# A searched order, an earlier z and reordered loads in a linear-attention and gMLP block

## The chip, the cores and the metric

The kernel runs on one core of one Trainium2 chip. A core has five engines that run side by side, each through its own list of instructions in order: TensorE (PE) for matmuls, VectorE (DVE), ScalarE (ACT), GpSimd (POOL), and SyncE (SP), which here only issues transfers. They wait for each other through semaphores. The metric is the device time of one execution in microseconds; the median of several runs counts.

## The reference

x has 2048 tokens of 512 values in bf16. Two blocks follow each other, each after a layer norm and with a residual sum.

```python
phi = lambda t: jnp.where(t > 0, t + 1, jnp.exp(t)) + 1e-06
# A: 32 heads of 16
pq, pk = phi(q), phi(k)                      # q, k, v = layernorm(x) @ wqkv
kv  = einsum('bhsd,bhse->bhde', pk, v)
z   = einsum('bhsd->bhd', pk)
o   = einsum('bhqd,bhde->bhqe', pq, kv) / (einsum('bhqd,bhd->bhq', pq, z) + 1e-06)
h   = x + o @ wo
# B
y   = gelu(layernorm(h) @ w_in)              # 1792 columns, two halves of 896
z1, z2 = y[..., :896], layernorm(y[..., 896:])
g   = einsum('ts,bsf->btf', w_sp, z2) + b_sp[None, :, None]
out = h + (z1 * g) @ w_out
```

The sum over all tokens in kv and z means that no q can be used before the last k is done; the spatial product with w_sp (2048 x 2048) means that no g can be computed before the last z2 is normalised.

## The kernel before

Tokens are cut into NT = 16 tiles of 128, and for some steps into NG = 4 groups of 512. The kernel is written as a list of operations with their reads and writes (`_Prog.add`). Nothing in the source fixes the order in which an engine runs them: dependencies come from the footprints in memory, and `schedule` makes an order by a model. Each operation has a cost and a latency in nanoseconds, written where it is added (for instance 167 and 535 for the two POOL steps of `rstd`, lines 501 and 503). `_pass` is a list scheduler: at each step the engine that can start first takes its ready operation of best rank. `schedule` (line 166) ranks by the longest path to the end, then alternates passes forward and backward in time (ROUNDS = 12) and keeps the shortest plan. `emit` writes each engine's list in that order, with the waits that the dependencies need. Source order still matters in one way: two operations that share a buffer are ordered as the source has them.

The stages, with the names that the profile shows:

- Loads. `load_x` and `load_w` issue transfers on the queues of SP and ACT (line 438): x in pieces of one or two tiles, the weights wk (keys) and wq (queries), each 512 KB. Each has a latency for the model. POOL makes constants, and ACT loads the table for Exp and Ln (line 459) with a priority of 9e5.
- Warm-up. `warmup(40)` runs 40 matmuls on zeros (line 547) while the first loads are under way.
- `k_unit(n)` takes two tiles: statistics on DVE (`stats`, lines 495 and 496), the reciprocal deviation on POOL (`rstd`), the normalisation into xn on DVE or ACT, a transpose into xnT on PE (line 527, the first six tiles) or by DMA (line 441), the K product into one of the two pairs of PSUM banks 0-1 and 2-3, which `next_pair` hands out in turn, and `phi` into pk (ACT Exp, line 427 "e"; DVE, lines 539 and 540). Then xn^T pk is summed over all tiles in banks 4 to 7 (line 589, list CB). This is the matrix C from which kv follows as wv^T C, so v itself is never made.
- `q_unit(tg, c)` makes two of four blocks of 128 query columns for one group of 512 tokens, in a pair from `next_pair`, with `phi` into pqT. There are eight of these units. QS says after which k_unit how many are written down; the rest follow the transition.
- Transition. C goes to SBUF (ct, line 620). z comes from sixteen small matmuls on pk (line 626), an ACT copy (zsum), eight small matmuls with a selector (line 647) and four DVE steps into zmat (line 651); it uses bank ZB = CB[0]. kv is made in bank CB[1] (line 636), masked to the heads (kvm), and multiplied by wo into m (banks 6, 7, 5, 4; line 658).
- Denominators. For every group and pair of blocks, zmat^T pqT goes to banks 6 and 7, ACT takes Ln and then Exp of the negative (line 427 "r", one buffer), and DVE multiplies pqT (line 672).
- h tiles. pqT^T m goes to banks 4 and 5; then x is added (line 683), and statistics, rstd, normalisation into hn and a transpose by DMA into hnT follow.
- z2 and z1. After the last denominator ACT loads the Gelu table (line 694). z2 of a tile is hnT^T win (lines 702 and 705), Gelu, its layer norm in DVE and POOL steps (lines 714 to 722, 513). z1T is 28 tiles of win^T hnT with Gelu, in banks 6 and 7.
- G and output. For each of four groups, seven products of z2 with the transposed w_sp (448 matmuls in all), bias and product with z1T (lines 763 and 765), and the output product with wout (line 753).

Of the kernel before, what the change touches and what calls it, by code (L numbers as in the profile page):

```python
# [6 lines left out]
ACT = mybir.ActivationFunctionType  # L7
ALU = mybir.AluOpType

P = 128  # L10
GRAN = 16
SEM_NS = 45.0
LOOK = 100.0
ROUNDS = 12


class _Op:
# [13 lines left out]
class _Prog:  # L31
# [98 lines left out]
    def _pass(self, rank, back):  # L130
# [32 lines left out]
                    cand[ops[u].eng].append(u)  # L163
        return start

    def schedule(self):
        ops = self.ops
        for o in ops:
            for d in o.deps:
                ops[d].users.append(o.i)  # L170
        for o in reversed(ops):
            o.prio = max((ops[u].prio + self._lag(o, ops[u]) for u in o.users), default=o.lat) + o.cost + o.bias
        rank = [-o.prio for o in ops]
        best = None
        for _ in range(ROUNDS):
            start = self._pass(rank, False)
            span = max(start[o.i] + o.cost + o.lat for o in ops)
            if best is None or span < best[0] - 1:
                best = (span, start)
            late = self._pass([-(start[o.i] + o.cost) for o in ops], True)  # L180
            rank = [-(late[o.i] + o.cost) for o in ops]
        self.est, self.start = best
        self.seq = sorted(ops, key=lambda o: (self.start[o.i], o.i))
        self.order = {e: [o for o in self.seq if o.eng == e] for e in self.ENGS}
# [91 lines left out]
def bass_sequential_preLN__linear_attn_block__mixer_gmlp__prompt_kernel(  # L276
# [11 lines left out]
    _, S, D = A_x.shape  # L288
# [4 lines left out]
    NT, KD, KF = S // P, D // P, FH // P  # L293
    GW = 512
# [6 lines left out]
    g = _Prog(nc)  # L301
# [37 lines left out]
    wqkv = g.sbuf("wqkv", o_wqkv, [KD, 3 * D], BF16)  # L339
# [4 lines left out]
    pk = g.sbuf("pk", o_pk, [NT, D], BF16)  # L344
# [12 lines left out]
    zsum = g.sbuf("zsum", o_r, [GW], FP32)  # L357
# [41 lines left out]
    def PE(fn, reads, writes, ns, **k):  # L399
        return g.add("PE", fn, reads, writes, cost=ns, lat=165, **k)  # L400
# [11 lines left out]
    def dve_cost(n, ps, acc=1):  # L412
        return n / acc / 0.96 + 58

    def act_cost(n, ps):
        return n / 1.2 + (49 if ps else 92)

    def act(out_ap, in_ap, func, n, bias=None, scale=None, extra=(), accum=None, **k):
        kw = {}
        if bias is not None:  # L420
            kw["bias"] = bias
        if scale is not None:
            kw["scale"] = scale
        if accum is not None:
            kw["accum_out"] = accum
        ps = in_ap.tensor.name == "psum"
        return g.add("ACT", lambda ac: ac.activation(out_ap, in_ap, func, **kw), [in_ap, *extra],  # L427
                     [out_ap] + ([accum] if accum is not None else []),
                     cost=act_cost(n, ps) + 93 * len(extra) + (92 if accum is not None else 0), lat=120, **k)

    def dve(fn, reads, writes, n, ps=False, acc=1, **k):
        return g.add("DVE", fn, reads, writes, cost=dve_cost(n, ps, acc), lat=95, **k)
# [4 lines left out]
    def dma(eng, out_ap, in_ap, name, issue=100.0, lat=2500.0, **k):  # L437
        return g.add(eng, lambda q: q.dma_start(out_ap, in_ap), [in_ap], [out_ap], cost=issue, lat=lat, dma=name, **k)

    def dma_t(out_ap, in_ap, name, issue=1310.0, lat=1600.0, **k):  # L440
# [15 lines left out]
                                   base=0, channel_multiplier=1), [bmask], [bmask], 350, bias=1e5)  # L456
    pool(lambda p: p.affine_select(bm3, bm3, pattern=[[DH, P // DH], [0, DH]], compare_op=ALU.is_gt, fill=0.0,
                                   base=DH, channel_multiplier=-1), [bmask], [bmask], 350, bias=1e5)
    g.add("ACT", lambda ac: ac.preload_act_table_set("natural_log_exp_and_others"), [], [], cost=1300, bias=9e5)


    later = [1e6]
# [1 line left out]
    def prio():  # L464
        later[0] -= 1e3
        return later[0]

    wq = A_wqkv.rearrange("(c p) f -> p c f", p=P)

    def load_w(eng, j, nm, lat):  # L470
        dma(eng, wqkv[:, :, j * D:(j + 1) * D], wq[:, :, j * D:(j + 1) * D], nm, issue=500, lat=lat, bias=prio())

    def load_x(eng, n, w, lat):
        dma(eng, x[:, n:n + w, :], x_d[n * P:(n + w) * P, :].rearrange("(n p) d -> p n d", p=P), f"x{n}", issue=500,
            lat=lat, bias=prio())
# [3 lines left out]

    load_x("SP", 0, 1, 2000)  # L480
    load_x("ACT", 1, 1, 2200)
    load_w("SP", 1, "wk", 4300)
    load_x("ACT", 2, 2, 3000)
    load_x("ACT", 4, 2, 4000)
    load_x("SP", 6, 2, 5500)
    load_x("ACT", 8, 2, 5000)
    load_x("SP", 10, 2, 6500)
    load_x("ACT", 12, 2, 6000)
    load_x("SP", 14, 2, 7500)
    load_w("ACT", 0, "wq", 9000)  # L490


    def stats(src, k, n):
# [40 lines left out]
    def phi(dst, b, w=2):  # L534

        e, t = e_t[ecnt[0] % NE][:, 0:w, :], psum[:, b:b + w, :]
        ecnt[0] += 1
        act(e, t, ACT.Exp, w * GW)
        dve(lambda v: v.tensor_scalar(e, e, 1.0, EPS_PHI, op0=ALU.min, op1=ALU.add), [e], [e], w * GW, acc=4)  # L539
        dve(lambda v: v.scalar_tensor_tensor(dst, t, 1.0 + EPS_PHI, e, op0=ALU.add, op1=ALU.max),  # L540
            [t, e], [dst], w * GW, ps=True)

    def warmup(n):
        def fn(pe):
            inst = None
            for _ in range(n):
                inst = pe.matmul(bank(7, P), lhsT=warm, rhs=warm, start=True, stop=True)
            return inst
        PE(fn, [warm], [bank(7, P)], n * 64, bias=1e6)

    warmup(40)

    PAIRS = [0, 2]
    pc = [0]

    def next_pair():
        pc[0] += 1
        return PAIRS[pc[0] % 2]

    CB = [4, 5, 6, 7]  # L560
# [34 lines left out]
    def q_unit(tg, c):  # L595
        b = next_pair()
        for i in (0, 1):
            matmuls(bank(b + i), [(wqkv[:, d, (c + i) * P:(c + i + 1) * P], xnT[:, d, tg * GW:(tg + 1) * GW])
                                  for d in range(KD)])
        phi(pqT[:, c:c + 2, tg * GW:(tg + 1) * GW], b)  # L600

    QS = {8: 1, 10: 1, 12: 2, 14: 2}
    qs = [(tg, c) for tg in range(NG) for c in range(0, KD, 2)]
    for n in range(0, NT, 2):
        k_unit(n)
        for _ in range(QS.get(n, 0)):
            q_unit(*qs.pop(0))

    for dst, src, nm in ((wqkv[:, :, 2 * D:3 * D], A_wqkv[:, 2 * D:3 * D], "wv"), (wo, A_wo, "wo"),
                         (win, B_w_in, "win"), (wout, B_w_out, "wout")):  # L610
        late = load("SP", dst, src, nm, 2000, issue=src.shape[0] * src.shape[1] * 2 / 350)
        late.deps.add(g.last.i)


    ZB, KVB = CB[0], CB[1]
    for c in range(KD):
        if c % 2:
            act(ct[:, c, :], bank(CB[c]), ACT.Copy, GW)
        else:
            dve(lambda v, c=c: v.tensor_copy(ct[:, c, :], bank(CB[c])), [bank(CB[c])], [ct[:, c, :]], GW, ps=True)  # L620

    def fn(pe):
        inst = None
        for i in range(NT // 4):
            for j in range(4):
                inst = pe.matmul(psum[32 * j:32 * (j + 1), ZB, :], lhsT=ones32, rhs=pk[:, 4 * i + j, :],
                                 start=i == 0, stop=i == NT // 4 - 1)
        return inst
    PE(fn, [ones32, pk], [bank(ZB)], NT // 4 * 300)
    act(zsum, bank(ZB), ACT.Copy, GW)  # L630

    def fn(pe):
        inst = None
# [6 lines left out]
    dve(lambda v: v.tensor_tensor(kvm, bank(KVB).rearrange("p (c t) -> p c t", c=KD),  # L640
                                  bmask.rearrange("p (c t) -> p c t", c=1).to_broadcast([P, KD, P]), ALU.mult),
        [bank(KVB), bmask], [kvm], GW, ps=True)

    def fn(pe):
        inst = None
        for c in range(KD):
            inst = pe.matmul(bank(ZB, 1, c), lhsT=zsum[:, c * P:(c + 1) * P], rhs=sel[:, 0:1], start=True, stop=True)
        return inst
    PE(fn, [zsum, sel], [bank(ZB)], KD * 250)
    for c in range(KD):  # L650
        dve(lambda v, c=c: v.tensor_scalar(zmat[:, c, :], bmask, bank(ZB, 1, c), None, op0=ALU.mult),
            [bmask, bank(ZB)], [zmat[:, c, :]], P)
    for c, b in zip(range(KD), (6, 7, 5, 4)):
        matmuls(bank(b), [(kvm[:, c, :], wo[:, c, :])])
        if c % 2:
            act(m[:, c, :], bank(b), ACT.Copy, GW)
        else:
            dve(lambda v, c=c, b=b: v.tensor_copy(m[:, c, :], bank(b)), [bank(b)], [m[:, c, :]], GW, ps=True)
# [21 lines left out]
    for n in range(NT):  # L680
        b = AB[n % 2]
# [14 lines left out]
    for n in range(NT):  # L696
        b = next_pair()
# [34 lines left out]
    for tg in range(NG):  # L732
        for fc in range(KF):
            b = Z1B[k % 2]
# [22 lines left out]
    for tg in range(NG):  # L757
        tok = slice(tg * GW, (tg + 1) * GW)
        for fc in range(KF):
            b = GB[(tg * KF + fc) % 2]  # L760
            matmuls(bank(b), [(z2[:, s, fc * P:(fc + 1) * P], wsp[:, s, tok]) for s in range(NT)])
            t, z = u_t[fc % 2], z1T[:, fc, tok]
# [37 lines left out]
```

## Time and profile before

| | |
|---|---|
| time, median of 3 runs | 260.2 us (260.05 to 260.46) |
| span in the profile | 258.9 us |
| PE busy | 243.6 us (94%) |
| DVE busy | 132.7 us (51%) |
| ACT busy | 86.6 us (33%) |
| POOL busy | 46.5 us (18%) |
| mean granted clock of PE | 0.98 |
| POOL rs L501, 128x1, mean | 258 ns |
| POOL rs L503, 128x1, mean | 604 ns |
| ACT Ln, Exp of a denominator, mean | 1114, 1058 ns |
| DVE pk/pqT L540, 128x1024, mean | 1225 ns |

The profile is of one execution. Busy time is the union of an engine's instructions; matmuls overlap, so that a record of a 128x512 matmul is 379 ns long where the next one starts after 216 ns. The chain of waits is the sequence of work that ended last, followed back from the end: at each step to what released it. The granted clock is the share of PE's full clock that was let through.

### The profile page before, as it was taken

To read this page: it belongs to the slowest core of one execution; us is meant where nothing else is said; L and a number is where in the kernel's file an instruction comes from. 1 tells how busy PE (TensorE), PEld (TensorE's weight loads), DVE (VectorE), ACT (ScalarE), POOL (GpSimd) and SP (SyncE) were. 2 spreads that over 40 slices of the span, in tenths; PEclk is the share of its full clock that TensorE was granted. 3 is DMA by queue.
4 is the path that set the end of the run, shared out by engine and by line. 5 is a ranking of instruction groups with operands and counts; after the bars stand their busy time and mean duration, and the time that the engine had idled before them with its cause. 6 is when DMAs were issued, how large, how long until landed. Compare 5 with 4: busy or idle time off the path is not lost.

```text
span 258.9 us, 3119 instructions
## 1 busy us (share of the span) xinstructions
PE 243.6 (94%) x1180; PEld 111.7 (43%) x1180; DVE 132.7 (51%) x270; ACT 86.6 (33%) x122; POOL 46.5 (18%) x134
## 2 busy tenths in 40 slices
PE   5698999995989999799999999999999999999995
PEld 5343444451334454344444444444444444444442
DVE  2998665587699999982322221414204211054063
ACT  1379633469689667561000001103003000000020
POOL 5345100000136887960000000000000000000000
PEclk9799999998699999999999999999999999999999
DMA  7813479943034444684544444000000000021012
GB/s 226 261 41 81 85 242 368 121 102 81 1 78 88 95 87 101 85 167 98 93 92 101 101 85 100 20 0 3 0 0 0 0 3 0 0 81 61 22 61 101
DMA packets 57166, 21.57 MB, mean 83 GB/s; under 512 B 49472, under 2 KB 56512, under 8 KB 57152
## 3 DMA queue, kind: packets, MB, share of 16 engines
q1 hardware_dynamic: 55392, 19.67, 32.9%
q10 hardware_dynamic: 1760, 1.70, 2.0%
q8 instruction: 9, 0.15, 0.2%
q14 instruction: 5, 0.04, 0.1%
HBM read 7.47 MB, written 2.10 MB: 37 GB/s over the span
## 4 chain that ended last, share of the span: by engine, by line
PE 67%; DVE 15%; POOL 8%; ACT 5%; DMA 2%; issue 2%; POOLq 0%; ACTq 0%
PE psum L408 62%; POOL rs L503 5%; DVE st L495 4%; PE psum L589 4%; DVE h L683 2%; POOL rs L501 2%; ACT r L427 2%; DMA x<-in_A_x_dram 2%; DVE pk L540 2%; DVE hn L513 2%; ACT e L427 2%; DVE st L720 1%; DVE st L721 1%; DVE z L513 1%; DVE st L496 1%
## 5 line engine op out<-in xcount | busy, mean ns | idle before, releaser
L408 PE MATMUL psum<-wsp,z 128*128 128x512 bf16 x448 | 98.2, 379 | 0.2 <-DVE z L513 0.2
L408 PEld LDWEIGHTS psum<-wsp,z 128*128 128x128 bf16 x448 | 43.7, 98 | 53.3 <-DVE z L513 0.7
L427 ACT ACTIVATE z1T<-psum 128x512 bf16<-128x512 f32 x28 | 16.7, 597 | 121.8 <-PE psum L408 121.8
L763 DVE TENSOR_TENSOR u<-psum,bsp 128x512 bf16<-128x512 f32 x28 | 19.2, 690 | 39.7 <-PE psum L408 39.4
L765 DVE TENSOR_TENSOR z1T<-u,z1T 128x512 bf16<-128x512 bf16 x28 | 11.6, 421 | 40.1 <-ACT z1T L427 39.7
L408 PE MATMUL psum<-hnT,win 128*128 128x512 bf16 x112 | 26.3, 379 | 0.0
L503 POOL TENSOR_TENSOR rs<-rs,expo 128x1 f32<-128x1 f32 (+1 forms) x41 | 25.7, 628 | 2.4
L408 PE MATMUL psum<-wout,z1T 128*128 128x512 bf16 x112 | 25.3, 379 | 0.0
L427 ACT ACTIVATE e<-psum 128x1024 bf16<-128x1024 f32 (+1 forms) x18 | 16.6, 926 | 17.1 <-PE psum L408 17.1
L501 POOL TENSOR_SCALAR rs<-st 128x1 f32<-128x1 f32 (+1 forms) x41 | 10.4, 255 | 65.2 <-DVE st L496 62.0
L753 DVE TENSOR_TENSOR ost<-psum,h 128x512 bf16<-128x512 f32 x16 | 10.2, 683 | 19.3 <-PE psum L408 19.3
L702 PE MATMUL psum<-win,hnT 128*128 128x512 bf16 x64 | 16.4, 379 | 2.1 <-DMA hnT<-hn 2.0
L408 PE MATMUL psum<-m,pqT 128*128 128x512 bf16 x64 | 17.7, 420 | 0.7 <-DVE h L683 0.6
L427 ACT ACTIVATE z<-psum 128x896 bf16<-128x896 f32 x16 | 14.6, 910 | 10.7 <-PE psum L705 10.6
L408 PE MATMUL psum<-wqkv,xnT 128*128 128x512 bf16 x64 | 16.5, 399 | 1.2 <-ACT xnT L427 1.0
L408 PEld LDWEIGHTS psum<-wout,z1T 128*128 128x128 bf16 x112 | 11.0, 98 | 13.2
L408 PE MATMUL psum<-xnT,wqkv 128*128 128x512 bf16 x64 | 15.6, 379 | 0.7 <-DVE pk L540 0.7
L589 PE MATMUL psum<-pk,xn 128*128 128x512 bf16 x64 | 16.1, 379 | 0.0
L408 PEld LDWEIGHTS psum<-hnT,win 128*128 128x128 bf16 x112 | 10.2, 98 | 13.7 <-ACT z1T L427 3.2
L705 PE MATMUL psum<-win,hnT 128*128 128x384 bf16 x64 | 13.0, 326 | 0.0
L539 DVE TENSOR_SCALAR e<-e 128x1024 bf16<-128x1024 bf16 (+1 forms) x18 | 7.2, 398 | 11.3 <-ACT e L427 11.2
L495 DVE BATCH_NORM_STATS2 st<-x 128x6 f32<-128x512 bf16 x16 | 10.4, 679 | 4.9 <-DMA x<-in_A_x_dram 4.9
(67 smaller groups left out, 203.5 us busy)
## 6 DMA issues: line engine op xcount, KB each, us to landing
out_dram<-ost SPq DMA_DIRECT2D x16, 128.0 KB, 1.7
win<-in_B_w_in_dram SPq DMA_DIRECT2D x1, 1792.0 KB, 11.3
x<-in_A_x_dram ACTq DMA_DIRECT2D x4, 256.0 KB, 7.1
wqkv<-in_A_wqkv_dram SPq DMA_DIRECT2D x2, 512.0 KB, 4.7
wsp<-in_B_w_sp_dram SPq DMA_TRANSPOSE x64, 2.8
wout<-in_B_w_out_dram SPq DMA_DIRECT2D x1, 896.0 KB, 7.3
x<-in_A_x_dram SPq DMA_DIRECT2D x3, 256.0 KB, 6.9
wqkv<-in_A_wqkv_dram ACTq DMA_DIRECT2D x1, 512.0 KB, 8.9
```

What stands on the lines that cost most here:

```text
L408: inst = pe.matmul(out_ap, lhsT=a, rhs=b, start=start and i == 0, stop=stop and i == len(pairs) - 1)
L427: return g.add("ACT", lambda ac: ac.activation(out_ap, in_ap, func, **kw), [in_ap, *extra], [out_ap] + ([accum] if accum is not None else []),
L495: dve(lambda v: v.bn_stats(s[:, 0:6], src[:, n, :]), [src[:, n, :]], [s[:, 0:6]], D)
L501: pool(lambda p: p.tensor_scalar(rr[:, :, 1:2], ss[:, :, col + 1:col + 2], EPS_LN, None, op0=ALU.add), [ss[:, :, col + 1:col + 2]], [rr], 167)
L503: pool(lambda p: p.tensor_tensor(rr[:, :, 0:1], rr[:, :, 1:2], expo[:, 0:w].rearrange("p (a b) -> p a b", b=1), ALU.pow), [rr, expo], [rr] ...
L513: dve(lambda v: v.tensor_scalar(dst, src, mean, rst, op0=ALU.subtract, op1=ALU.mult), [src, mean, rst], [dst], w + 460, acc=4)
L589: inst = pe.matmul(bank(CB[c]), lhsT=xn[:, i, c * P:(c + 1) * P], rhs=pk[:, i, :], start=i == 0, stop=i == NT - 1)
L702: pe.matmul(bank(b), lhsT=hnT[:, c, n * P:(n + 1) * P], rhs=win[:, c, FH:FH + GW], start=c == 0, stop=c == KD - 1)
L705: inst = pe.matmul(bank(b + 1, F2), lhsT=hnT[:, c, n * P:(n + 1) * P], rhs=win[:, c, FH + GW:F], start=c == 0, stop=c == KD - 1)
L753: dve(lambda v: v.tensor_tensor(o, bank(b), h[:, n, :], ALU.add), [bank(b), h[:, n, :]], [o], D, ps=True)
L763: dve(lambda v, t=t, b=b, tok=tok: v.tensor_tensor(t, bank(b), bsp[:, tok], ALU.add), [bank(b), bsp[:, tok]], [t], GW, ps=True)
L765: dve(lambda v, t=t, z=z: v.tensor_tensor(z, t, z, ALU.mult), [t, z], [z], GW, acc=2)
```

## The change

There are five edits.

1. Search. `schedule` runs 20 alternations from the longest-path rank (`_swing`), then ROUNDS = 400 trials. Each adds normal noise (200 to 3000 ns) to the planned start times of the best plan, in a window of 5 to 40 us or, in 4 cases of 10, over the whole plan, and alternates twice from there. A plan is judged by `_value`: its length plus half of what each gap between PE operations has over 800 ns.
2. z. The steps of z become `z_unit`, in a pair from `next_pair`, written after the last k_unit and the q unit that follows it, which is the fourth. QS goes from 1, 1, 2, 2 to 1, 1, 1, 1, so that four q units and not two are written after the transition. kv takes CB[0], m the banks 5 and 4 in turn.
3. Loads. x tiles 2 and 3 are loaded singly, wk is loaded in two halves, one on each queue, after x tiles 0 to 3, and the other x loads and wq follow, most on SP. The model's latencies are set as measured.
4. The table load for Exp and Ln has no priority any more and stands after the loads.
5. The warm-up has 56 matmuls, with a model cost of 2200 + 54 a matmul in place of 64 a matmul.

```diff
-ROUNDS = 12
+ROUNDS = 400
...
+    def _value(self, start):
+
+        v = max(start[o.i] + o.cost + o.lat for o in self.ops)
+        last = None
+        for t, c in sorted((start[o.i], o.cost) for o in self.ops if o.eng == "PE"):
+            if last is not None and t - last > 800:
+                v += (t - last - 800) * 0.5
+            last = t + c
+        return v
...
-        for _ in range(ROUNDS):
-            start = self._pass(rank, False)
-            span = max(start[o.i] + o.cost + o.lat for o in ops)
-            if best is None or span < best[0] - 1:
-                best = (span, start)
-            late = self._pass([-(start[o.i] + o.cost) for o in ops], True)
-            rank = [-(late[o.i] + o.cost) for o in ops]
+        best = self._swing([-o.prio for o in ops], 20)
+        rng = np.random.default_rng(0)
+        for _ in range(ROUNDS):
+            t = np.array(best[1])
+            a, w = rng.uniform(0, 0.6 * best[0]), rng.uniform(5e3, 4e4)
+            if rng.random() < 0.4:
+                a, w = 0.0, best[0]
+            near = (t >= a) & (t < a + w)
+            got = self._swing(list(t + near * rng.normal(0, rng.choice([200, 600, 1500, 3000]), len(ops))), 2)
+            if got[0] <= best[0]:
+                best = got
...
-    g.add("ACT", lambda ac: ac.preload_act_table_set("natural_log_exp_and_others"), [], [], cost=1300, bias=9e5)
...
     load_x("SP", 0, 1, 2000)
     load_x("ACT", 1, 1, 2200)
-    load_w("SP", 1, "wk", 4300)
-    load_x("ACT", 2, 2, 3000)
-    load_x("ACT", 4, 2, 4000)
-    load_x("SP", 6, 2, 5500)
-    load_x("ACT", 8, 2, 5000)
-    load_x("SP", 10, 2, 6500)
-    load_x("ACT", 12, 2, 6000)
-    load_x("SP", 14, 2, 7500)
-    load_w("ACT", 0, "wq", 9000)
+    load_x("SP", 2, 1, 2700)
+    load_x("ACT", 3, 1, 2900)
+    for eng, c in (("SP", 0), ("ACT", 2)):
+        dma(eng, wqkv[:, c:c + 2, D:2 * D], wq[:, c:c + 2, D:2 * D], f"wk{c}", issue=500, lat=3600, bias=prio())
+    load_x("SP", 4, 2, 4600)
+    load_x("ACT", 6, 2, 4800)
+    for n, t in ((8, 5100), (10, 5600), (12, 6100), (14, 6700)):
+        load_x("SP", n, 2, t)
+    load_w("SP", 0, "wq", 7500)
+    preload = g.add("ACT", lambda ac: ac.preload_act_table_set("natural_log_exp_and_others"), [], [], cost=1300)
...
-        PE(fn, [warm], [bank(7, P)], n * 64, bias=1e6)
+        PE(fn, [warm], [bank(7, P)], 2200 + n * 54, bias=1e6)
 
-    warmup(40)
+    warmup(56)
...
+    def z_unit():
+
+        zb = next_pair()
...
+        PE(fn, [ones32, pk], [bank(zb)], NT // 4 * 260)
+        act(zsum, bank(zb), ACT.Copy, GW)
...
+        PE(fn, [zsum, sel], [bank(zb + 1)], KD * 250)
+        for c in range(KD):
+            dve(lambda v, c=c: v.tensor_scalar(zmat[:, c, :], bmask, bank(zb + 1, 1, c), None, op0=ALU.mult),
+                [bmask, bank(zb + 1)], [zmat[:, c, :]], P)
...
-    QS = {8: 1, 10: 1, 12: 2, 14: 2}
+    QS = {8: 1, 10: 1, 12: 1, 14: 1}
     qs = [(tg, c) for tg in range(NG) for c in range(0, KD, 2)]
     for n in range(0, NT, 2):
         k_unit(n)
-        for _ in range(QS.get(n, 0)):
+        for i in range(QS.get(n, 0)):
             q_unit(*qs.pop(0))
+            if n == NT - 2 and i == 0:
+                z_unit()
...
-    ZB, KVB = CB[0], CB[1]
+    KVB = CB[0]
...
-    for c, b in zip(range(KD), (6, 7, 5, 4)):
+        b = CB[1 - c % 2]
         matmuls(bank(b), [(kvm[:, c, :], wo[:, c, :])])
```

More of the change, by code (lines that the diff above doesn't have):

```diff
@@ L164, in _pass, with _swing @@
         return start
+    def _value(self, start):
[6 more added lines that the diff above has]
+        return v
+    def _swing(self, rank, n):
+        best = None
+        for _ in range(n):
+            start = self._pass(rank, False)
+            v = self._value(start)
+            if best is None or v < best[0]:
+                best = (v, start)
+            late = self._pass([-(start[o.i] + o.cost) for o in self.ops], True)
+            rank = [-(late[o.i] + o.cost) for o in self.ops]
+        return best
     def schedule(self):
@@ L172, in schedule @@
             o.prio = max((ops[u].prio + self._lag(o, ops[u]) for u in o.users), default=o.lat) + o.cost + o.bias
-        rank = [-o.prio for o in ops]
-        best = None
+        best = self._swing([-o.prio for o in ops], 20)
+        rng = np.random.default_rng(0)
         for _ in range(ROUNDS):
-            start = self._pass(rank, False)
-            span = max(start[o.i] + o.cost + o.lat for o in ops)
-            if best is None or span < best[0] - 1:
-                best = (span, start)
-            late = self._pass([-(start[o.i] + o.cost) for o in ops], True)
-            rank = [-(late[o.i] + o.cost) for o in ops]
+            t = np.array(best[1])
[6 more added lines that the diff above has]
+                best = got
         self.est, self.start = best
@@ L600, in q_unit, with fn @@
         phi(pqT[:, c:c + 2, tg * GW:(tg + 1) * GW], b)
-    QS = {8: 1, 10: 1, 12: 2, 14: 2}
+    def z_unit():
+        zb = next_pair()
+        def fn(pe):
+            inst = None
+            for i in range(NT // 4):
+                for j in range(4):
+                    inst = pe.matmul(psum[32 * j:32 * (j + 1), zb, :], lhsT=ones32, rhs=pk[:, 4 * i + j, :],
+                                     start=i == 0, stop=i == NT // 4 - 1)
+            return inst
+        PE(fn, [ones32, pk], [bank(zb)], NT // 4 * 260)
+        act(zsum, bank(zb), ACT.Copy, GW)
+        def fn(pe):
+            inst = None
+            for c in range(KD):
+                inst = pe.matmul(bank(zb + 1, 1, c), lhsT=zsum[:, c * P:(c + 1) * P], rhs=sel[:, 0:1], start=True,
+                                 stop=True)
+            return inst
+        PE(fn, [zsum, sel], [bank(zb + 1)], KD * 250)
+        for c in range(KD):
+            dve(lambda v, c=c: v.tensor_scalar(zmat[:, c, :], bmask, bank(zb + 1, 1, c), None, op0=ALU.mult),
+                [bmask, bank(zb + 1)], [zmat[:, c, :]], P)
+    QS = {8: 1, 10: 1, 12: 1, 14: 1}
     qs = [(tg, c) for tg in range(NG) for c in range(0, KD, 2)]
@@ L620, in bass_sequential_preLN__linear_attn_block__mixer_gmlp__prompt_kernel @@
             dve(lambda v, c=c: v.tensor_copy(ct[:, c, :], bank(CB[c])), [bank(CB[c])], [ct[:, c, :]], GW, ps=True)
[L622 to L630, printed above, removed]
     def fn(pe):
@@ L642, in bass_sequential_preLN__linear_attn_block__mixer_gmlp__prompt_kernel @@
         [bank(KVB), bmask], [kvm], GW, ps=True)
[L644 to L649, printed above, removed]
     for c in range(KD):
-        dve(lambda v, c=c: v.tensor_scalar(zmat[:, c, :], bmask, bank(ZB, 1, c), None, op0=ALU.mult),
-            [bmask, bank(ZB)], [zmat[:, c, :]], P)
-    for c, b in zip(range(KD), (6, 7, 5, 4)):
+        b = CB[1 - c % 2]
         matmuls(bank(b), [(kvm[:, c, :], wo[:, c, :])])
```

## The prediction

> **What bounds the kernel now.** I read the page first (busy shares, the 40 slices, the chain), then PE alone in order of time, then the busy time by stretch, then the waits.
>
> The page's slices show where TensorE (PE) is not full and where its clock is low:
>
> ```profile
> PE   5698999995989999799999999999999999999995
> DVE  2998665587699999982322221414204211054063
> ACT  1379633469689667561000001103003000000020
> POOL 5345100000136887960000000000000000000000
> PEclk9799999998699999999999999999999999999999
> ```
>
> A slice is 6.47 us. From slice 18 (117 us) on, PE is full at full clock. The holes lie before: slices 0 and 1, slices 9 and 10, slice 16. In slices 1 and 10 the clock is down to 0.7 and 0.6. VectorE (DVE) is full in slices 1 to 3 and 11 to 16.
>
> The late part of the chain of waits, read in order of time, is one piece of PE:
>
> ```profile
> 117.09 0.52 DVE z L513
> 117.66 138.32 PE psum L408 x640
> 256.00 0.69 DVE ost L753
> ```
>
> 640 matmuls in 138.32 us are 0.216 us each: the pace of a 128x512 matmul at full clock (a row's mean of 379 ns overlaps its neighbours). Nothing in the change touches this part, so the question is what PE loses before 117.66. PE's own timeline, the front:
>
> ```profile
> 1.73 3.79 PE L547 MATMUL psum<-warm 128*128 128x128 bf16 x40 [1.73 <-POOL warm L445]
> 8.04 1.04 PE L527 MATMUL psum<-ident,xn 128*128 128x128 bf16 x8 [2.52 <-DVE xn L513]
> 9.34 2.94 PE L408 MATMUL psum<-wqkv,xnT 128*128 128x512 bf16 x8 [0.26 <-ACT xnT L427]
> ```
>
> The warm-up ends at 5.52, the first real work comes at 8.04, and the first eight K matmuls take 2.94 us where the pace gives 8 x 0.216 = 1.73: they run mostly at half clock. The cause of the late start is in the general timeline:
>
> ```profile
> 6.38 1.28 DVE L495 BATCH_NORM_STATS2 st<-x 128x6 f32<-128x512 bf16 x2 [1.56 <-DMA x<-in_A_x_dram]
> 7.59 0.72 DVE L513 TENSOR_SCALAR xn<-x,st,rs 128x512 bf16<-128x512 bf16 x2
> ```
>
> DVE stands 1.56 us for the load of x tiles 2 and 3 while tile 0's normalisation is queued behind; its reciprocal deviation was ready near 5.7 (POOL L503 begins at 5.13, two of 0.55). The middle, again PE alone:
>
> ```profile
> 57.91 1.89 PE L408 MATMUL psum<-xnT,wqkv 128*128 128x512 bf16 x8
> 60.18 0.60 PE L408 MATMUL psum<-pqT,zmat 128*128 128x512 bf16 x2 [0.38 <-ACT r L427]
> 63.52 1.03 PE L408 MATMUL psum<-pqT,zmat 128*128 128x512 bf16 x2 [2.74 <-ACT r L427]
> 64.35 3.62 PE L408 MATMUL psum<-m,pqT 128*128 128x512 bf16 x8
> ```
>
> Here the Ln and Exp of the denominators (L427 "r") hold banks 6 and 7, PE has nothing else queued, and afterwards eight matmuls take 3.4 us from start to next start: half clock. The stretches confirm it:
>
> ```profile
> 59.00:63.50 4.50, 1.41 (x6) 0.30 (x4) 3.93 (x6) 4.47 (x6) 0.00 (x0) 0.91 0.51 114
> 63.50:68.00 4.50, 4.48 (x11) 1.64 (x12) 1.38 (x2) 3.23 (x3) 0.00 (x0) 0.50 0.02 3
> ```
>
> (Columns: length, busy PE, PE weight load, DVE, ACT, POOL, then clock.) In the first ACT is full and PE is not; in the second the clock is 0.50.
>
> Sum of PE's losses between 8.04 and 117.66, each as elapsed minus count x 0.216 (0.056 for a transpose, eight of which take 0.45 from 16.06): front until 14.33, 6.29 - 16 x 0.056 - 12 x 0.216 = 2.8; gaps at 22.6, 30.4 and 30.8, 1.3; the middle from 59.6 to 80.8, 0.5 + 2.9 + 2.7 (fifteen cold matmuls, 5.95 against 3.24) + 1.8 of small gaps = 7.9; gaps at 102.0, 107.4 and 117.3, 2.7. Together 14.7 us, the most that an order of work can win, besides an earlier start.
>
> **What the Trainium skill says.** "TensorE: Matmul & The Clock Gate", Part 1, says that PE starts at half clock, goes to full after about 3.4 us of sustained work, and falls back after about 3.4 us of idleness, by a free-running window. The trace agrees roughly: 2.52 us idle at the front and 2.91 us at 60.6 were each followed by half clock. The same page (engine queue depths) calls DVE and ACT strict in order; DVE's queued normalisation above behaves so. "DMA: Bandwidth & Descriptors", Issuing engines are not separate DMA queues, says that transfers issued by several engines share 16 DMA engines, and only issue time is saved: so halves of wk on two queues are no faster as bytes; the order of bytes is what counts. "ScalarE: Activation LUTs", What ACT_TABLE_LOAD costs, gives 1283 ns for a load; the trace has 1.28 us.
>
> **The change part by part.**
>
> Loads. x tiles 2 and 3 become single 128 KB loads ahead of wk, so 512 KB of x are first. The front moved 226 to 264 GB/s; single loads landed 2.5 and 2.7 us after issue, the 256 KB ones 7 us. I estimate tiles 2 and 3 near 4.5 us, when DVE has just finished the first two statistics (3.32 + 1.29), and wk (1 MB in all) near 6, before it is needed. DVE's 1.56 us stand goes. Transposes at about 6.4 instead of 8.04, first K at about 7.2. The rest of x lands by about 11 (2.5 MB at 250 GB/s), ahead of DVE, which takes 1.3 us of statistics per pair; wq was needed at 23.46. These are hidden by DVE work.
>
> Table load without priority. ACT ran it from 4.64 to 5.92 after six issues and first computes at 8.69. Four issues now stand before it: it stays hidden in that idle time. Nothing.
>
> Warm-up 40 to 56. Its matmuls start from 1.73 to 5.3, and the shortest records (219 ns against a median of 314) show the clock rising at the end, so sixteen more cost about 0.056 each: the end moves from 5.52 to about 6.4, into the idle time before the transposes. PE then stays warm. It saves 1.2 us on eight K matmuls and 0.4 on transposes, but DVE is full there (15.37 of 15.66 us in 9.34 to 25), so only part counts. From front and warm-up together I take DVE's stands, 1.56 plus some of the DVE waits from PE: **2.0 us**; bounds 1.0 and 3.5.
>
> z in a K slot, QS 8,10,12,14 of 1 each instead of 1,1,2,2. The work of z is the same: 16 matmuls in 0.98 us, one evacuation of 0.60, 8 small in 0.95, four DVE of 0.25. It is now written behind the last k unit and the fourth q unit and needs no C bank, so zmat, hence the first Ln, no longer follows the evacuation of C. Added wait: z takes a slot of the rotating K pairs, so the sixth q unit, which gets that pair next, waits for z's last DVE step, and PE's list stands behind it. With the fifth unit in the other pair and C's last tiles (0.86 us each) to lay between, I cost this at nothing, at most the 1.9 us of z itself. Two more q units (8 x 0.216 = 1.73 us of PE each) come after the transition: that is 3.45 us of PE work for the hole of 2.9 + 0.5. Their ACT (1.02 each) and DVE (0.43 + 1.23) work moves too and is the price: ACT has 8 x (1.11 + 1.06) = 17.4 us of Ln and Exp there. m is now evacuated from banks 4 and 5, not 6 and 7, so the denominators no longer share banks with it; before, m's last evacuation sat at 61.86 behind ACT work although its matmul ran at 57.69.
>
> Search. 400 random perturbations replace 12 rounds; a PE gap over 0.8 us costs half its excess extra. It can use what the old order left: q units in the middle, and z1 matmuls (only 32 of 112 run before 117.66) in the late gaps. But its costs are optimistic: Ln on PSUM is planned at 995 ns and measures 1107, a POOL pair at 167 + 535 and measures 258 + 604. So I give it half of the middle, 7.9 / 2 = **3.9 us** (bounds 0 and 6.5), and **0.8** of the late 2.7 (bounds -2 and 2). DVE, full from 68 on, is why not more: in the chain a tile of h costs it 0.60 + 0.60 + 0.09 + 0.33 before PE's next stage can start.
>
> Sum: 2.0 + 3.9 + 0.8 = 6.7; 260.2 - 6.7 = **253.5 us**.
>
> **The rivals.** *Front only*: ACT's chain of Ln and Exp sets the middle whatever PE does; ACT is 4.47 of 4.50 full there, which speaks for it; that 3 us of q units were run earlier speaks against. 260.2 - 2.0 = 258.2. *Nearly gapless*: the search finds z1 and q units for almost all holes, and clock loss vanishes: 2.0 + 6.5 + 2.0 = 10.5, 249.7. For it: the spare 80 z1 matmuls; against: DVE full in slices 11 to 16, and in-order queues on optimistic costs. *Slower*: an order tuned closer to the model breaks on it. 32 POOL pairs are 0.16 us over plan; if half reach the path, 2.6 us, plus 7 chains of four small POOL steps at 0.33 over, 2.3, and the front's 2.0 off: 263.1. Against: the old order was made with the same costs, and POOL was already in its chain.
>
> **How the numbers follow.** Forecast (251 to 256.5) 0.53; front only 0.20; nearly gapless 0.15; slower 0.12. The likeliest gives 253.5. The range 249.3 to 259.2 takes in the first three but their outer tails and leaves out the slower case. Faster 0.86, within 0.2% 0.03, slower 0.11.
>
> **What would show it.** Right: no DVE stand for x after 3.3 us, transposes near 6.4, K at about 1.73 us for eight; no PE gap over 2 us between 45 and 75 and PEclk at 9 there; G's first matmul near 111. Wrong: a new PE gap behind z or Ln with clock 0.5, or DVE and PE stands on POOL L503 growing past those of before.

## The result and the profile after

The changed kernel takes 249.9 us (median of 4; 249.1 to 252.59) against 260.1 us before: a ratio of 0.963, with a 95% interval of 0.9554 to 0.9705. The profiled span went from 258.9 to 248.0 us. Three of the four executions took 249.1 to 250.05 us at a mean clock of 1.0; the fourth, 252.59 us, had 0.993.

The slices of the page, which are now 6.2 us long:

```profile
PE   8899999999999999998999999999999999999994
DVE  3998565689999998482233322332123201443064
ACT  2588533699985679861000000000021000010020
POOL 5356000001125889751000000000000000000000
PEclk9999999999999999999999999999999999999999
```

PE has no hole left from slice 2 on but a shallow one in slice 18 (the last slice is the output's tail), and the clock is full throughout in this execution. DVE is as full as before in slices 9 to 14. The last part of the chain of waits:

```profile
112.84 0.52 DVE z L537
113.41 131.51 PE psum L432 x608
244.94 0.69 DVE ost L785
```

(L408 of before is L432 here, L513 is L537.) The 448 matmuls of G begin 4.25 us earlier, and 608 and not 640 matmuls are left from there on. The missing 32 are z1: 64 of its 112 now lie before 113.41, where 32 did. At 0.216 us they are the other 6.9 us of the 11 by which PE ends sooner.

PE alone in order of time, the front:

```profile
1.22 5.58 PE L571 MATMUL psum<-warm 128*128 128x128 bf16 x56 [1.22 <-POOL warm L469]
6.93 0.72 PE L551 MATMUL psum<-ident,xn 128*128 128x128 bf16 x8
8.58 1.02 PE L432 MATMUL psum<-wqkv,xnT 128*128 128x512 bf16 x4 [0.93 <-ACT xnT L451]
```

And two lines of DVE from the general timeline, ahead of those transposes:

```profile
5.86 0.69 DVE L519 BATCH_NORM_STATS2 st<-x 128x6 f32<-128x512 bf16 x1 [0.31 <-DMA x<-in_A_x_dram]
6.47 0.72 DVE L537 TENSOR_SCALAR xn<-x,st,rs 128x512 bf16<-128x512 bf16 x2
```

The transposes start 1.1 us earlier, and four K matmuls take 1.02 us: full clock. DVE's stand for x has shrunk from 1.56 to 0.31 us, but the statistics of tile 3 (at 5.86) are still queued ahead of tile 0's normalisation.

The middle, PE alone (the count and busy time of each group; no bracket means that PE did not stand):

```profile
43.94 1.05 PE L634 MATMUL psum<-pk,ones 128*32 128x512 bf16 x16
...
47.51 0.61 PE L432 MATMUL psum<-pqT,zmat 128*128 128x512 bf16 x2
47.95 1.06 PE L677 MATMUL psum<-ct,wqkv 128*128 128x128 bf16 x16
...
53.17 1.90 PE L432 MATMUL psum<-xnT,wqkv 128*128 128x512 bf16 x8
54.90 0.38 PE L432 MATMUL psum<-pqT,zmat 128*128 128x512 bf16 x1
55.54 1.04 PE L432 MATMUL psum<-xnT,wqkv 128*128 128x512 bf16 x4 [0.26 <-DVE pqT L564]
56.41 1.03 PE L432 MATMUL psum<-m,pqT 128*128 128x512 bf16 x4
```

The same steps of the kernel before, PE alone:

```profile
50.75 1.05 PE L626 MATMUL psum<-pk,ones 128*32 128x512 bf16 x16
51.73 1.07 PE L636 MATMUL psum<-ct,wqkv 128*128 128x128 bf16 x16
...
54.89 0.59 PE L408 MATMUL psum<-pqT,zmat 128*128 128x512 bf16 x2
```

The sums of z run at 43.94 in place of 50.75. The first denominator product runs at 47.51, before kv is made (the group with ct); before, it ran at 54.89, after kv and half of m. Query units fill what ACT needs for Ln and Exp. The first h product comes at 56.41 and not at 64.35. The stretches from z to the first h product, and from there (columns as in the prediction):

```profile
43.94:56.41 12.47, 12.21 (x83) 5.89 (x83) 10.25 (x18) 10.18 (x14) 0.00 (x0) 1.00 0.43 95
56.41:65.37 8.96, 8.96 (x41) 3.64 (x40) 8.93 (x17) 8.59 (x9) 1.69 (x4) 1.00 0.50 93
65.37:80.66 15.29, 15.29 (x75) 7.01 (x74) 15.21 (x35) 11.31 (x16) 5.31 (x17) 1.00 0.47 102
```

In the second, PE is busy for all of 8.96 us, DVE for 8.93 and ACT for 8.59: three engines are full at once. PE's losses, counted as in the prediction, fell from 14.7 to 4.9 us: 1.9 until 20.53, 0.1 until 43.94, 1.2 until 80.66, 1.7 until 113.41. These 9.8 us and the start that is 1.1 us earlier make up the whole 10.9 us of the span.

### The profile page after: what moved, and what is told of

The parts are those of the page before. It is cut to its first block, busy times and chain, and to the rows that moved or that the text cites. A ratio compares the mean times of both kernels' runs of the same rounds, so it can differ in the third digit from the quotient of the medians.

```text
span 248.0 us, 3139 instructions
## 1 busy us (share of the span) xinstructions
PE 240.6 (97%) x1196; PEld 111.9 (45%) x1196; DVE 133.1 (54%) x270; ACT 86.2 (35%) x122; POOL 44.6 (18%) x134
## 4 chain that ended last, share of the span: by engine, by line
PE 65%; DVE 18%; POOL 8%; ACT 4%; issue 2%; DMA 2%; SPq 0%; POOLq 0%
PE psum L432 60%; POOL rs L527 5%; DVE st L519 5%; PE psum L613 4%; DVE h L715 4%; POOL rs L525 2%; ACT r L451 2%; DMA x<-in_A_x_dram 2%; DVE pqT L704 1%; DVE pk L564 1%; ACT e L451 1%; DVE z L537 1%; DVE pqT L564 1%; DVE hn L537 1%; DVE st L752 1%
## 5 line engine op out<-in xcount | busy, mean ns | idle before, releaser
L432 PE MATMUL psum<-wsp,z 128*128 128x512 bf16 x448 | 97.7, 379 | 0.8 <-DVE z L537 0.8
L432 PEld LDWEIGHTS psum<-wsp,z 128*128 128x128 bf16 x448 | 43.7, 98 | 54.0 <-DVE z L537 1.3
L432 PE MATMUL psum<-hnT,win 128*128 128x512 bf16 x112 | 26.5, 379 | 0.0
L432 PE MATMUL psum<-wout,z1T 128*128 128x512 bf16 x112 | 25.7, 379 | 0.0
L527 POOL TENSOR_TENSOR rs<-rs,expo 128x1 f32<-128x1 f32 (+1 forms) x41 | 25.1, 621 | 1.8
L525 POOL TENSOR_SCALAR rs<-st 128x1 f32<-128x1 f32 (+1 forms) x41 | 9.3, 233 | 60.5 <-DVE st L520 56.7
L432 PE MATMUL psum<-wqkv,xnT 128*128 128x512 bf16 x64 | 15.7, 379 | 1.4 <-ACT xnT L451 0.9
L432 PEld LDWEIGHTS psum<-wout,z1T 128*128 128x128 bf16 x112 | 10.9, 98 | 13.4 <-DVE ost L785 0.6
L432 PEld LDWEIGHTS psum<-hnT,win 128*128 128x128 bf16 x112 | 10.2, 98 | 13.4 <-ACT z1T L451 2.8
L432 PE MATMUL psum<-xnT,wqkv 128*128 128x512 bf16 x64 | 15.8, 379 | 0.3 <-DVE pqT L564 0.3
L432 PE MATMUL psum<-m,pqT 128*128 128x512 bf16 x64 | 15.7, 380 | 0.0
```

What stands on the lines that cost most here:

```text
L432: inst = pe.matmul(out_ap, lhsT=a, rhs=b, start=start and i == 0, stop=stop and i == len(pairs) - 1)
L525: pool(lambda p: p.tensor_scalar(rr[:, :, 1:2], ss[:, :, col + 1:col + 2], EPS_LN, None, op0=ALU.add), [ss[:, :, col + 1:col + 2]], [rr], 167)
L527: pool(lambda p: p.tensor_tensor(rr[:, :, 0:1], rr[:, :, 1:2], expo[:, 0:w].rearrange("p (a b) -> p a b", b=1), ALU.pow), [rr, expo], [rr] ...
```

## The experiments

Theory A was that the search and the four q units left over for the middle need each other; the rivals were that the search alone (B) or z and QS alone (C) close the hole.

**1. Everything but the search.** The whole `schedule` is that of before.

```diff
-ROUNDS = 400
+ROUNDS = 12
...
-        best = self._swing([-o.prio for o in ops], 20)
+        rank = [-o.prio for o in ops]
+        best = None
```

> The changed kernel with the old schedule function (12 alternations, plain length): loads, z in a K slot, QS, warm-up and table load as changed. Theory A (the middle hole closes only if q units are left for it and the search puts them there): the front's gain and half of the middle at most, 255 to 257.5 us, with PE gaps of 2 us or more left in the middle. Rival B (the search alone closes it): 258 us or more. Rival C (z and QS alone close it, whatever the order): 251 to 252.5 us, no PE gap over 1 us between 43 and 65.

Measured: 259.31 us, ratio 0.9971 (0.9947 to 0.9995). The hole at the denominators is gone, and yet the kernel is hardly faster. Its PE stands somewhere else, as its timeline shows:

```profile
24.88 3.62 PE L408 MATMUL psum<-wqkv,xnT 128*128 128x512 bf16 x16
30.47 3.38 PE L408 MATMUL psum<-wqkv,xnT 128*128 128x512 bf16 x8 [1.97 <-DVE pk L540]
33.65 1.27 PE L589 MATMUL psum<-pk,xn 128*128 128x512 bf16 x4
```

A K unit's `phi` holds PE for 1.97 us, and the eight matmuls behind it take 3.18 us until the next start, nearly half clock: 4 us lost between 28 and 35. In all PE loses 15.0 us before G by the same count as above, as much as before. The sums of z run at 44.35, about where they run in the changed kernel (43.94), but the first denominator product stands in PE's list only at 52.28 and the first h product at 64.29. By the count, PE loses 5.6 us from z to 81 and not 7.9 as before, but 7.1 us ahead of z and not 4.2. C falls, and A with it, which expected 255 to 257.5 here: what the edits gain in the middle, this plan loses at the front.

**2. The search alone**, on the kernel before (the diff of experiment 1 the other way round).

> The kernel before with only the new search (400 trials, penalty on PE gaps). Theory A: 255 to 257.5 us, because only two q units are left for the hole and the front is late as before. Rival B: 251 to 253 us, the middle and late gaps gone. Rival C: 258.5 to 260.5 us.

Measured: 253.02 us, ratio 0.9746 (0.9693 to 0.9799): 7.1 us of the 10.2. That is at the edge of what B expected; A falls. The late gaps are gone, as B had it, the middle's are not. Where it still loses, PE alone:

```profile
55.89 0.38 PE L432 MATMUL psum<-wo,kvm 128*128 128x512 bf16 x1
56.11 1.89 PE L432 MATMUL psum<-xnT,wqkv 128*128 128x512 bf16 x8
58.38 0.61 PE L432 MATMUL psum<-pqT,zmat 128*128 128x512 bf16 x2 [0.38 <-ACT r L451]
60.53 1.90 PE L432 MATMUL psum<-m,pqT 128*128 128x512 bf16 x8 [1.55 <-DVE pqT L696]
```

The first h product comes 3.8 us earlier than before and still stands 1.55 us for a normalised pqT, behind ACT's Ln and Exp. The profile has 89 z1 matmuls on record before G here (a few records are missing), against 32 before, and no late gap of 0.3 us is left. By the count, PE loses 3.9 us from z to 81 (7.9 before) and next to nothing from there to G (2.7 before). This profile is of the fastest of the four executions, 251.89 us.

**3 and 4. The warm-up by itself**, in both kernels, with the order untouched because the plan still holds the same cost.

Number 3, on the changed kernel:

```diff
-            for _ in range(n):
+            for _ in range(40):
```

Number 4, on the kernel before:

```diff
-            for _ in range(n):
+            for _ in range(56):
```

> The changed kernel in its own order, but with 40 warm-up matmuls issued where the plan holds 56: only the warm-up differs. Theory A (the warm-up matters): PE idles about 1.8 us before the transposes at 6.9, the first K matmuls go at half clock and the kernel takes 0.7 to 1.7 us more, 250.6 to 251.6. Rival D (DVE is full there and hides PE's clock): within 0.4 us of the changed kernel, 249.5 to 250.3, though the first K matmuls are slow.

> The kernel before in its own order with 56 warm-up matmuls: only the warm-up differs. Theory A: the first eight K matmuls take 1.73 us in place of 2.94 and the kernel 0.7 to 1.5 us less, 258.7 to 259.5. Rival D: DVE hides it, 259.8 to 260.4.

Measured: number 3, 252.08 us (249.23, 252.05, 252.1, 252.71), ratio 0.9685 (0.9626 to 0.9743); number 4, 259.81 us, ratio 0.9991 (0.9971 to 1.0011). In the profile of 4, PE alone, the front is warm (seven of the eight K matmuls are recorded, in 1.67 us) and the hole of the middle is where it was:

```profile
8.95 1.67 PE L408 MATMUL psum<-wqkv,xnT 128*128 128x512 bf16 x7 [0.59 <-ACT xnT L427]
...
63.19 0.60 PE L408 MATMUL psum<-pqT,zmat 128*128 128x512 bf16 x2 [2.75 <-ACT r L427]
```

So in the old order a warm front gives nothing that the time shows; by the interval, up to 0.8 us is not excluded. The profile of 3 is of its fastest execution, and its front is warm too: with 40 matmuls PE stands only 0.96 us before the transposes, and these take 0.72 us as in the changed kernel.

```profile
6.64 0.72 PE L551 MATMUL psum<-ident,xn 128*128 128x128 bf16 x8 [0.96 <-DVE xn L537]
7.73 1.04 PE L432 MATMUL psum<-wqkv,xnT 128*128 128x512 bf16 x3 [0.37 <-ACT xnT L451]
```

The other three executions of 3 are 2.8 to 3.5 us slower, and no profile shows what differs in them. In the new order 40 against 56 stays open: the intervals of 3 and of the changed kernel overlap.

**5. z, QS and the banks of kv and m as before**, all else as changed.

```diff
-    QS = {8: 1, 10: 1, 12: 1, 14: 1}
+    QS = {8: 1, 10: 1, 12: 2, 14: 2}
...
-        b = CB[1 - c % 2]
+    for c, b in zip(range(KD), (6, 7, 5, 4)):
```

> The changed kernel (new search, loads and warm-up) with z, QS and the banks of kv and m as before. Theory E (the search gains most, and z and QS give it room for the last few us of the middle): 251.5 to 254 us, a gap of 1 us or more before a denominator matmul near 60. Rival F (z and QS add nothing once the search runs): 249 to 251 us.

Measured: 255.62 us, ratio 0.9807 (0.9752 to 0.9862). The price, 5.7 us, is higher than E had it, and F falls. It is not a matter of the clock: the two executions at a mean clock of 1.0 took 254.7 us, those of the changed kernel 249.1 to 250.05. PE alone:

```profile
52.95 0.60 PE L432 MATMUL psum<-pqT,zmat 128*128 128x512 bf16 x2
...
58.16 0.60 PE L432 MATMUL psum<-pqT,zmat 128*128 128x512 bf16 x2 [0.17 <-ACT r L451]
60.32 1.90 PE L432 MATMUL psum<-m,pqT 128*128 128x512 bf16 x8 [1.55 <-DVE pqT L696]
```

The same stand of 1.55 us for pqT as in experiment 2, 0.2 us apart in time, although the searches took different ways. By the count PE loses 4.1 us from z to 81, against 1.2 in the changed kernel. That is some 3.0 of the 5.4 us by which its start and its losses exceed the changed kernel's; the rest lies at the front (1.3) and after 81 (1.1), and the traces do not show that z is its cause.

**6. The loads as before**, in order, sizes, queues and planned latencies.

```diff
-    load_x("SP", 2, 1, 2700)
-    load_x("ACT", 3, 1, 2900)
+    load_w("SP", 1, "wk", 4300)
+    load_x("ACT", 2, 2, 3000)
...
```

> The changed kernel with the order, sizes, queues and planned latencies of the loads as before (the table load stays where the change has it). Theory E: the front is later by what DVE stands for x tiles 2 and 3, the first transposes near 7.7 in place of 6.9 and 0.7 to 1.5 us more in all, 250.6 to 251.5 us. Rival G (the front is hidden by DVE's later work): 249.5 to 250.3 us.

Measured: 249.92 us, ratio 0.9602 (0.9548 to 0.9656): G. DVE does stand longer, and the transposes start at 7.67 and not at 6.93, at no cost that the time shows. From the general timeline:

```profile
6.01 1.29 DVE L519 BATCH_NORM_STATS2 st<-x 128x6 f32<-128x512 bf16 x2 [0.96 <-DMA x<-in_A_x_dram]
7.67 0.85 PE L551 MATMUL psum<-ident,xn 128*128 128x128 bf16 x8 [0.32 <-DVE xn L537]
```

**7. Another seed** (`default_rng(2)`).

> The changed kernel with the random numbers of the search started from seed 2. Theory E (any search of 400 trials finds such an order): within 1 us of the changed kernel, 249 to 251 us. Rival H (seed 0 was a lucky order): 251.5 us or more.

Measured: 250.18 us, ratio 0.9593 (0.9541 to 0.9644): E. Seed 0 was no lucky draw, as far as one other seed can show it.

**8. z in the K slot, but the q units as before.**

```diff
-    QS = {8: 1, 10: 1, 12: 1, 14: 1}
+    QS = {8: 1, 10: 1, 12: 2, 14: 2}
```

> The changed kernel with z in the K slot, kv and m in the new banks, but the q units as before: 1, 1, 2, 2 before the transition, two after. Theory J (where z and m lie is what counts, since the denominators stop waiting for their banks): 249.5 to 252 us. Rival K (the q units left for the hole count): 253 us or more, with a gap of 1 us or more before 65.

Measured: 251.7 us (249.7 to 252.93), ratio 0.969 (0.9613 to 0.9767). J holds and K falls: z and m in their new places take most of the way from 255.6 without the q units left over. All four executions lie below all four of experiment 5, but the intervals just overlap. What the q units left over add, 1.8 us in the medians, lies inside the intervals.

**9. The old z, but m in banks 5 and 4.**

```diff
-    for c, b in zip(range(KD), (6, 7, 5, 4)):
+    for c, b in zip(range(KD), (5, 4, 5, 4)):
```

> The old place of z (and the old q units) with the new search and loads, but m's four products go to banks 5, 4, 5, 4 instead of 6, 7, 5, 4, so that the denominators have banks 6 and 7 to themselves. If the shared banks are what the old z cost: 251 to 253 us, against 255.6 with the old banks. If it is that zmat comes too late: 254.5 to 256.5 us, no better.

Measured: 253.96 us, ratio 0.978 (0.9721 to 0.9839), between the two expectations and not told apart from experiment 5. PE's stand before the first h product shrinks, another stays (PE alone):

```profile
60.05 1.90 PE L432 MATMUL psum<-m,pqT 128*128 128x512 bf16 x8 [0.62 <-DVE pqT L696]
...
66.24 1.04 PE L432 MATMUL psum<-m,pqT 128*128 128x512 bf16 x4 [1.32 <-DVE pqT L696]
```

Freeing banks 6 and 7 does not move the first h product (60.05 against 60.32). With z in the slot it came at 57.16 (experiment 8). By the count, PE loses 2.8 us from z to 81 here, but also 5.0 us ahead of z (2.0 in the changed kernel): over half of the distance to the changed kernel is made before z, and the traces do not show that the place of z is the cause of it.

**10. No price on PE gaps** (`v += 0.0`, with seed 1; for seed 0 there is no time).

> The changed kernel with the price of a PE gap over 800 ns set to zero in the judging of a plan, and random seed 1. Theory E (the plan's length alone drives PE's gaps out, since PE is the bound): 249 to 251 us. Rival I (the price keeps the clock up): gaps of 2 us and half clock come back, 251.5 to 254 us.

Measured: 251.01 us, ratio 0.9667 (0.9609 to 0.9726); the clock stays full in every slice and no PE gap in the middle reaches 1 us. Rival I falls, which expected gaps of 2 us; whether the price is worth the 1.1 us of the medians is left open.

**11. One warm-up matmul**, in the changed kernel's own order.

```diff
-            for _ in range(n):
+            for _ in range(1):
```

> The changed kernel in its own order with one warm-up matmul in place of 56. If a cold start is paid in full: the first 16 K matmuls and the transposes run at half clock for some 3.4 us, 1.7 us more or, with what waits behind, up to 3: 251.5 to 253 us. If DVE hides it: 249.5 to 250.5 us.

Measured: 251.85 us (251.38 to 252.17), ratio 0.9705 (0.9634 to 0.9775). The front is cold:

```profile
7.32 1.04 PE L551 MATMUL psum<-ident,xn 128*128 128x128 bf16 x8 [5.80 <-DVE xn L537]
8.61 1.89 PE L432 MATMUL psum<-wqkv,xnT 128*128 128x512 bf16 x4 [0.26 <-ACT xnT L451]
```

Four K matmuls take 1.89 us in place of 1.02. The kernel is 1.95 us slower by the medians, though the intervals overlap and the slowest execution of the changed kernel (252.59) is slower than all four of these. In the profiled execution x tile 3 also landed 0.4 us later. So some 2 us is the best figure for a warm-up as a whole in the new order, and it is not clear of noise.

**12. Planned costs as in the trace**, to see whether better costs would win the rest.

```diff
-             [ss[:, :, col + 1:col + 2]], [rr], 167)
+             [ss[:, :, col + 1:col + 2]], [rr], 200)
...
-                                       expo[:, 0:w].rearrange("p (a b) -> p a b", b=1), ALU.pow), [rr, expo], [rr], 535)
+                                       expo[:, 0:w].rearrange("p (a b) -> p a b", b=1), ALU.pow), [rr, expo], [rr], 590)
...
-    load_x("SP", 2, 1, 2700)
-    load_x("ACT", 3, 1, 2900)
+    load_x("SP", 2, 1, 3100)
+    load_x("ACT", 3, 1, 4100)
```

(The small POOL steps of z2 are planned at 230 ns in place of 167, and the seed is 1. The planned Ln stays at 995 ns.)

> The changed kernel with planned costs nearer to the trace: POOL steps 200 and 590 ns in place of 167 and 535, the small POOL steps of z2 at 230, and x tiles 2 and 3 due 0.4 and 1.2 us later, as they landed; random seed 1. If the plan's optimistic costs are what leaves the last 4 to 6 us of PE loss: 247 to 249 us, first K matmul before 8.0. If not: 249.3 to 251 us, no different from the changed kernel.

Measured: 249.99 us, ratio 0.9609 (0.9586 to 0.9633), no different from the changed kernel. The first K matmuls do start earlier, at 7.93, and the time is lost again just behind, since the next tiles of x have not landed. From its general timeline:

```profile
7.93 1.89 PE L432 MATMUL psum<-wqkv,xnT 128*128 128x512 bf16 x8 [0.27 <-DMA wqkv<-in_A_wqkv_dram]
9.00 1.29 DVE L519 BATCH_NORM_STATS2 st<-x 128x6 f32<-128x512 bf16 x2 [1.71 <-DMA x<-in_A_x_dram]
```

No version is faster than the changed kernel by more than the noise.

**What the runs say together.** Three starts in each profile (us), PE's losses by the count of the prediction, and the median time. "Lost, z to 81" runs from the sums of z to about 81 us; the last but one column is the start of the first transposes plus all of PE's losses up to G, with missing records filled in.

| kernel | first Ln | first h product | Gelu table load | lost, z to 81 | start + all losses | time |
|---|---|---|---|---|---|---|
| before | 56.0 | 64.4 | 78.4 | 7.9 | 22.9 | 260.1 |
| 1, all but the search | 52.9 | 64.3 | 77.6 | 5.6 | 23.3 | 259.3 |
| 5, old z | 54.0 | 60.3 | 77.8 | 4.1 | 17.1 | 255.6 |
| 9, old z, m in 5 and 4 | 54.2 | 60.1 | 75.8 | 2.8 | 16.3 | 254.0 |
| 2, search alone (old z) | 54.2 | 60.5 | 74.8 | 3.9 | 14.5 | 253.0 |
| 8, slot, old q units | 50.7 | 57.2 | 73.3 | 2.5 | 13.3 | 251.7 |
| 10, no price on gaps | 48.9 | 55.9 | 72.3 | 2.2 | 13.1 | 251.0 |
| 7, seed 2 | 51.2 | 58.5 | 74.8 | 1.3 | 13.6 | 250.2 |
| 12, measured costs | 49.7 | 57.0 | 73.4 | 1.7 | 12.2 | 250.0 |
| 6, old loads | 48.7 | 56.0 | 72.5 | 1.7 | 12.1 | 249.9 |
| changed | 48.2 | 56.4 | 71.5 | 1.2 | 11.7 | 249.9 |

The first h product sorts the kernels in three groups: about 64 goes with 260, about 60 with 253 to 256, 56 to 58.5 with 250 to 252. Within the last group it does not sort them: with seed 2 it comes 2.6 us later than in experiment 10, and the kernel is no slower. What accounts for the time in every row is the last but one column: in each profile the span less this sum is 235.7 to 236.3 us. So a kernel is faster here by what PE loses less, wherever it loses it, and an early h product is one way to lose less.

All six orders of the new search with z in the slot (the changed kernel, 6, 7, 8, 10, 12) have medians from 249.9 to 251.7, and all three with the old z from 253.0 to 255.6. That the edit of z and the banks is worth something under the new search is shown by these groups. How much is less sure: each edit also gives the search another order, and these differ at the front, too. That z works by way of an earlier chain of Ln and Exp is read from the starts in the table; no run moves that chain by itself.

## Why the prediction was right, and where it was off

The direction and the range held, the range with 0.6 us to spare; the point, 253.5, was 3.6 us too high. The forecast to which I gave 0.53, 251 to 256.5, did not come. What came, in the number, is the rival called nearly gapless, to which I gave 0.15. That the result lies in the range is owed to this rival's place in it.

*Loads.* The mechanism was half right: DVE's stand shrank from 1.56 to 0.31 us. The start that I expected at 6.4 came at 6.93, and K at 8.58 in place of 7.2, because tile 3 landed at 5.86 and not near 4.5, and its statistics were ordered ahead of tile 0's normalisation; PE then stood another 0.93 us for xnT. In experiment 6 none of it shows in the time. Of the 2.0 us that I gave to front and warm-up together, the loads earn nothing that a run shows.

*Table load.* Hidden, as said: it ran at 2.75, and ACT stood idle from its end until 7.36.

*Warm-up.* The front stayed warm, as forecast. Its time is not to be seen in the old order (experiment 4) and some 2 us, not clear of noise, in the new one (11). By the count the whole front won 3.3 us where I said 2.0: 1.1 from the earlier start, and PE's losses ahead of z fell from 4.2 to 2.0. The search has a part in this (3.0 in experiment 2 with it alone, 7.1 in experiment 1 without it); no run separates it from the loads and the warm-up.

*Search.* "I give it half of the middle, 7.9 / 2 = 3.9 us" was about right for the search by itself: in experiment 2 the middle's loss fell from 7.9 to 3.9. Late, where I gave it 0.8, it won 2.7 in that order and 1.0 in the changed one (2.7 to 1.7), through the z1 matmuls that the prediction named.

*z and QS.* This is the mis-sized term. The price of the added wait, nothing, held: no stand behind z shows in PE's list. But nothing was also all that I gave the edit in the sum. The middle's loss fell by 6.7 us, from 7.9 to 1.2, and not by 3.9; with the search but the old z it stays at 3.9 (experiment 2) or 4.1 (5). So z, the banks and QS together won 2.7 to 3.0 us there, in single profiles. I argued for the edit as room for q units (3.45 us of PE work for a hole of 3.4), and experiment 8 shows that z's new place, with the new banks, does most of it without them. The line that zmat no longer follows C's evacuation was there; I gave it no value.

*The two reasons for caution.* "Its costs are optimistic": experiment 12 plans with costs of POOL and loads nearer to the trace and gains nothing that shows, so these are not what limits the order. The planned Ln of 995 ns, which measures 1107 or more, was left as it is and stays untested. "DVE, full from 68 on, is why not more": DVE is still full from 56 to 80 (8.93 of 8.96 and 15.21 of 15.29 us in the stretches), and PE loses 0.5 us there. So a full DVE does not by itself leave PE idle. Only eight matmuls of q and z1 run on PE in that time; the rest are denominators, h products and z2, so it is, as far as PE's list shows, their own order and no filling that keeps PE busy there. Filling counts further on: of the 80 spare z1 matmuls (17.3 us, against 14.7 us of loss, all in my own numbers) 32 more ran before G.

*The clock.* I counted 4.3 us of PE loss to half clock before (2.7 in the middle, 1.6 at the front). Four of 39 executions of the kernel before ran at a mean clock of 0.999 and took 258.3 to 258.4 us against 260.1: by this, half clock was worth some 1.8 us of the time, and the rest of the gain is standing time. This is an estimate: a cold front does not show in the mean clock (see the last section), so these executions may still have had one.

## What to carry to other kernels

Where one engine is the bound, add up its losses and ask for each whether ready work for it exists elsewhere in its list; if it does, a better order can win much of it (here 9.8 of 14.7 us), even beside a second full engine. A structural edit and the order that uses it are to be tried together: here the edits without the search were worth 0.8 us and the search without them 7.1, together 10.2, though the 2.3 us between are not clear of the noise. It is worth a try, though not proven here, to look for the start of the slowest serial chain in the middle (here eight Ln and Exp pairs, 17.4 us) and to move what it waits for ahead of everything that it does not need.

## What the runs showed of the hardware

In the profile of experiment 1 a stand of PE of 1.97 us was followed by half clock, in experiment 2 one of 1.55 us was not. Both are shorter than the 3.4 us of idleness with which the prediction reckoned. Twenty executions of experiment 1's kernel, one and the same program, fell into two sets: ten with a mean clock of 0.999 or more took 257.7 to 259.0 us, ten at 0.993 took 259.6 to 260.9. So the same order can run 2 us faster or slower, with half clock in one case and without it in the other; no profile of the faster set was taken.

The 39 executions of the kernel before have mean clocks of 0.980, 0.985 to 0.987, 0.993 or 0.999, and none between. The steps are about 0.0065, and of a span of 259 us at half clock that is 0.0065 x 2 x 259 = 3.4 us: by this estimate half clock comes in pieces of one length, each of which takes up to 1.7 us of PE's time.

A mean clock of 1.0 does not say that the front was warm. The page of experiment 11 shows a full clock in every slice, and yet its first four K matmuls took 1.89 us in place of 1.02. Whether a front is cold has to be read from the pace of the matmuls.
